# Re-planning a fused attention and two-layer gated network on one core: new lock rules, new matmul prices, new priorities

## The chip, the cores and the metric

The kernel runs on one core of a Trainium2 chip. The metric is the device time of one launch in microseconds (us), taken as the median of the runs. The engines are PE (TensorE; PEld is its weight load), DVE (VectorE), ACT (ScalarE), POOL (GpSimd) and SP (SyncE), which here issues the DMAs. Each engine works through its own instructions in program order.

## The reference

Three layers follow one another, in float32. B is 4, H is 8, S is 576, D is 64, the model width is 512 and the inner width is 1024.

```python
# 1: attention; heads 0 to 3 see the last 32 keys, heads 4 to 7 every fourth of the last 128
scores = np.where(masks, q @ k.T / 8, -1e9)
x = softmax(scores) @ v                      # (B, S, 512)
# 2: token shift, squared relu, gate
xk = mu_k * x + (1 - mu_k) * x_prev; xr = mu_r * x + (1 - mu_r) * x_prev
x = sigmoid(xr @ w_r) * (np.maximum(xk @ w_k, 0) ** 2 @ w_v)
# 3: spatial gate
h = np.maximum(x @ w_in, 0); u, v = h[..., :512], h[..., 512:]
v_s = einsum('ts,bsd->btd', w_spatial, layernorm(v)) + b_spatial
out = (u * v_s) @ w_out
```

## The kernel before

The four batches b go through attention in two halves each: `att(b, 0)` for the four plain heads, `att(b, 1)` for the four dilated ones. A half is cut into blocks of 32 queries by 64 keys, 18 blocks in the plain half and 20 in the dilated one, so 38 blocks in a batch, and three groups of them (6 or 8 blocks) form one softmax step: score matmuls (`scores`, four small float32 matmuls to a block, one for each head), a mask, maximum, subtraction, exponential, sum, reciprocal and product on DVE, ACT and POOL, then transposes and `values` on PE. In batch 0 every third score block is led by a matmul whose result nobody uses (`keep_warm`). A float32 matmul leaves two records in the trace, so 48 records of scores are 24 matmuls, or 6 blocks; 20 records of values are 5 groups.

Layer 2 takes a batch in two halves of 288 tokens (`moe1_k`, `moe1_r`, `moe1_v`), layer 3 a batch at a time (`moe2`). Their products run as three float32r matmuls to a term: high by high, high by low, low by high. The splits into high and low parts (`halves`, `split`, tiles xh and xl, kh and kl, gh and gl) are a copy on ACT or DVE and a subtraction on DVE or POOL. In batch 0 the first product uses w_k whole, in plain float32; w_k is split later (`split_whole`). Weights come as 64-bit words and are turned into float32 by two ACT instructions and one of DVE (`split_weight`), 512 KB to a load.

The order of all this is written by a planner that runs on the host before the program is built. Every piece of work is an `add(...)` with its cost on each engine that may do it, what it reads and writes, and whether it is a DVE instruction that competes with POOL (`two`, lines 194 on). `schedule` (lines 221 on) simulates the engines: it picks among the pieces that are ready the one with the lowest priority number, and puts it on the engine where it ends first, with a penalty for DVE or POOL. `begin` and `until` (lines 258 and 264) model the competition between DVE and POOL. `tuned` makes the priority from the table `TUNE`: for the k-th of n pieces of one kind it is the piece's own due number, plus the table's first entry, plus its second times k/n; the last two entries of four are the penalties in ns for DVE and for POOL.

`order` then walks through the planned PE work: where the plan has PE empty for over 60 ns in its first 100 us, it fills the hole with bf16 matmuls of ones (fillers; tile names const-bfloat16-1.0). The program issues everything in the planned order, so a plan that is wrong about a duration does not break the result, but an engine then waits for the next instruction of its queue while others further back could run. All engine instructions are issued through one helper, so all have line 453 in the profile; the tile names tell them apart.

Of the kernel before, what the change touches and what calls it, by code (L numbers as in the profile page):

```python
# [36 lines left out]
def blocks(dil):  # L37
# [39 lines left out]
    ('nat', 0): {'nat': (-290891, -21190, 792, 22)},  # L77
    ('nat', 1): {'nat': (-99107, 59817, 792, 22)},
    ('nat', 2): {'nat': (-2719, -33639, 792, 22)},
    ('nat', 3): {'nat': (6890, -14597, 792, 22)},  # L80
    ('nat', 4): {'nat': (6134, 3634, 792, 22)},
    ('out', 0): {'egh': (-5837, -69306, 792, -800), 'egl': (-4485, -5835, -200, 300), 'ot': (-6470, -41169, -200, 22), 'out': (-3506, -12993, 792, 22), 'psB': (4616, 30510, 792, 22)},
    ('out', 1): {'egh': (-5605, 46828, 400, -800), 'egl': (-9221, 34856, -600, -800), 'ot': (-5825, 55324, -200, 22), 'out': (-573, -83659, 792, 22), 'psB': (-3029, 10154, 792, 22)},
    ('out', 2): {'egh': (-6267, 4285, -600, 800), 'egl': (-4284, -14269, 1500, 22), 'ot': (-7057, -70234, -600, 22), 'out': (338, -35004, 792, 22), 'psB': (-6791, -32635, 792, 22)},
    ('out', 3): {'egh': (-10401, -19476, 400, 0), 'egl': (-6940, 7231, 0, 300), 'ot': (-13264, -90296, 792, 22), 'out': (-7211, 6394, 792, 22), 'psB': (-13665, 52592, 792, 22)},
# [27 lines left out]
    ('start',): {'ident': (2016, -146136, 792, 22), 'identb': (6831, -68258, 792, 22), 'mask': (5734, -40694, 400, 22), 'mask2': (-265553, -66203, 792, 22), 'pt': (1829, 75005, 200, 2000), 'xok': (8400, -23780, 792, 22)},  # L113
# [55 lines left out]
class Plan:  # L169
# [51 lines left out]
    def schedule(self, prio):  # L221
# [42 lines left out]
        def until(e, i, t, c):  # L264
# [6 lines left out]
            if h <= t:  # L271
                return t + c
# [1535 lines left out]
```

## Time and profile before

| what | us |
|---|---|
| median of 3 runs | 589.58 (586.85 to 592.04) |
| the profiled execution's own time | 587.68 |
| its span, first to last instruction | 585.9 |
| PE busy | 569.7 (97%), of which fillers 18.4 |
| DVE busy | 353.0 (60%) |
| ACT busy | 253.0 (43%) |
| POOL busy | 123.5 (21%) |

PE is busy nearly all the time, but the fillers count as busy, so the share alone does not say how much work is left to be moved. Read it by stage: up to about 12 us PE can only wait for the first inputs, up to 150 us attention of batches 0 and 1 and the preparation of weights run beside the first products, and from 150 us on PE works nearly without a break. The profile also gives the granted clock of TensorE for every stretch.

### The profile page before, as it was taken

What the parts mean: (1) busy time and instruction counts of PE and PEld (TensorE: products, weight loads), DVE (VectorE), ACT (ScalarE), POOL (GpSimd) and SP (SyncE); (2) the same over time, 40 slices, a digit from 0 to 9 for tenths busy, and PEclk for the clock granted to TensorE, in tenths of its full rate; (3) what the DMA queues carried; (4) which work ended last, traced back from release to release, by engine and by line L of the source; (5) the groups of instructions that cost most, each with busy time, mean ns of one, the idle gap of its engine ahead of it and who ended that gap; (6) DMA issues with size and microseconds to landing.
All of it is one profiled execution on the core that took longest, in us unless ns stands there. A gap on an engine that the chain in (4) does not pass through costs nothing.

```text
span 585.9 us, 12550 instructions
## 1 busy us (share of the span) xinstructions
PE 569.7 (97%) x5171; PEld 508.7 (87%) x5171; DVE 353.0 (60%) x745; ACT 253.0 (43%) x566; POOL 123.5 (21%) x146
## 2 busy tenths in 40 slices
PE   9999998998999999999999999999999999999996
PEld 5666786787989999999999999988988988889995
DVE  2889998898784779561616122789344616634440
ACT  4697845554263475734526162085123012303231
POOL 1313214345112211110400010042005301420030
PEclk9999999998999999999999999999999999999999
DMA  9999955687621444000000010230011001001002
GB/s 180 232 227 231 271 101 104 129 120 112 130 61 26 107 144 145 21 0 1 1 1 2 1 46 0 68 111 23 1 37 37 0 19 55 18 2 37 36 1 90
DMA packets 99513, 42.92 MB, mean 73 GB/s; under 512 B 86208, under 2 KB 92352, under 8 KB 99456
## 3 DMA queue, kind: packets, MB, share of 16 engines
q1 hardware_dynamic: 99456, 42.13, 32.3%
q8 instruction: 40, 0.66, 0.5%
q14 instruction: 17, 0.14, 0.1%
HBM read 37.39 MB, written 4.72 MB: 72 GB/s over the span
## 4 chain that ended last, share of the span: by engine, by line
PE 80%; DVE 11%; DMA 4%; SPq 2%; issue 2%; ACT 1%; POOL 0%; DVEq 0%; ACTq 0%; POOLq 0%
PE psM L453 55%; PE psB L453 15%; PE psT L453 7%; PE psS L453 2%; DMA ld<-in_k_dram 2%; SPq L453 2%; DVE st L453 1%; DVE pr L453 1%; DVE kT L453 1%; DMA raw<-in_moe_w_out_dram 1%; DVE xm L453 1%; DVE tmp L453 1%; DVE xd L453 1%; DVE sq_dt.float32r L453 1%; DVE qT L453 1%
## 5 line engine op out<-in xcount | busy, mean ns | idle before, releaser
L453 PE MATMUL psM<-xh,wk 128*128 128x288 f32 x512 | 122.0, 328 | 0.3 <-DVE x L453 0.3
L453 PE MATMUL psM<-sq_dt.float32r,wv 128*128 128x288 f32 x768 | 114.3, 299 | 0.2 <-DVE wv L453 0.2
L453 PEld LDWEIGHTS psM<-sq_dt.float32r,wv 128*128 128x128 f32 x768 | 105.4, 189 | 2.6 <-ACT x L453 0.7
L453 PEld LDWEIGHTS psM<-xh,wk 128*128 128x128 f32 x512 | 87.2, 188 | 8.6 <-DVE x L453 1.2
L453 PE MATMUL psM<-xh,wr 128*128 128x288 f32 x256 | 62.1, 303 | 2.4 <-ACT kr L453 1.4
L453 PE MATMUL psM<-x2h,wi 128*128 128x288 f32 x256 | 57.6, 298 | 0.0
L453 PE MATMUL psM<-xl,wk 128*128 128x288 f32 x192 | 56.6, 295 | 0.0
L453 DVE TENSOR_TENSOR sq_dt.float32r<-kr,sq_dt.float32r 128x288 fp32r<-128x288 f32 x57 | 29.1, 512 | 36.8 <-ACT sq_dt.float32r L453 36.5
L453 PEld LDWEIGHTS psM<-xh,wr 128*128 128x128 f32 x256 | 44.3, 189 | 4.6 <-ACT kr L453 2.4
L453 PEld LDWEIGHTS psM<-x2h,wi 128*128 128x128 f32 x256 | 43.1, 188 | 1.9 <-ACT u L453 1.1
L453 ACT ACTIVATE u<-psM 128x288 f32<-128x288 f32 x27 | 11.1, 411 | 76.2 <-PE psM L453 74.7
L453 ACT ACTIVATE kr<-psM 128x288 f32<-128x288 f32 x51 | 20.9, 410 | 48.8 <-PE psM L453 46.0
L453 POOL TENSOR_TENSOR xl<-xm,xh 128x288 fp32r<-128x288 f32 x23 | 20.1, 879 | 96.3 <-DVE xh L453 80.2
L453 PE MATMUL psB<-wi,x2h 128*128 128x512 f32 x128 | 40.4, 397 | 0.0
L453 PE MATMUL psB<-wo,gh 128*128 128x512 f32 x128 | 39.9, 393 | 0.0
L453 PE MATMUL psM<-wsh,vl 128*128 128x288 f32 x128 | 38.0, 297 | 1.1 <-DVE vl L453 1.1
L453 PE MATMUL psM<-x2l,wi 128*128 128x288 f32 x128 | 37.8, 295 | 0.9 <-DVE eps L453 0.9
L453 PE MATMUL psM<-xl,wr 128*128 128x288 f32 x128 | 38.1, 298 | 0.2 <-DVE xl L453 0.2
L453 PE MATMUL psM<-wsh,vh 128*128 128x288 f32 x128 | 38.0, 297 | 0.0
L453 PE MATMUL psM<-wsl,vh 128*128 128x288 f32 x128 | 37.7, 295 | 0.0
L453 PEld LDWEIGHTS psM<-xl,wk 128*128 128x128 f32 x192 | 36.1, 188 | 0.0
L453 DVE SCALAR_TENSOR_TENSOR xm<-xd,mu,x 128x288 f32<-128x288 f32 x56 | 32.1, 595 | 5.7 <-POOL xl L453 5.1
(155 smaller groups left out, 1119.6 us busy)
## 6 DMA issues: line engine op xcount, KB each, us to landing
vw<-in_v_dram SPq DMA_DIRECT2D x36, 128.0 KB, 3.1
room<-in_moe_w_k_dram SPq DMA_DIRECT2D x8, 512.0 KB, 9.4
room<-in_moe_w_v_dram SPq DMA_DIRECT2D x8, 512.0 KB, 6.0
raw<-in_moe_w_in_dram SPq DMA_DIRECT2D x8, 512.0 KB, 3.8
out_dram<-ot SPq DMA_DIRECT2D x16, 256.0 KB, 2.0
ld<-in_q_dram SPq DMA_DIRECT2D x48, 72.0 KB, 2.6
ld<-in_k_dram SPq DMA_DIRECT2D x48, 72.0 KB, 3.2
vw<-in_v_dram SPq DMA_DIRECT2D x8, 288.0 KB, 5.5
```

The lines of the kernel that those rows point to most:

```text
L453: return self.tc.keep_in_program_order(getattr(self.engine, name)(*args, **kw))
```

## The change

Three things change in the planner; no instruction of the program is added, taken away or reshaped, except that fillers, which engine a piece goes to, and the order follow from the plan.

First, the competition of DVE and POOL: before, the later of two overlapping instructions ran on at 0.4 (POOL) or 0.35 (DVE) of its speed; some kinds ("both") waited for POOL to end. Now every DVE instruction marked `two` starts no sooner than 56 ns ahead of the end of the POOL instruction in hand, and a POOL instruction no sooner than 130 ns ahead of the end of such a DVE instruction. Second, a block of scores is put at 130 ns instead of 190 (batches 1 to 3) and 160 instead of 260 (batch 0), a group of values at 146 instead of 155. Third, all 109 entries of the table of priorities and penalties have new numbers.

```diff
         def begin(e, i):
             t = max(free[e], at[i])
-            if e == "dve" and two[i] == "both":
-                t = max(t, held["pool"])
+            if e == "dve" and two[i]:
+                t = max(t, held["pool"] - 56)
+            elif e == "pool" and i not in self.far:
+                t = max(t, held["dve"] - 130)
             return t
 
         def until(e, i, t, c):
-            if e == "pool":
-                h, rate = held["dve"], 0.4
-            elif e == "dve" and two[i]:
-                h, rate = held["pool"], 0.35
-            else:
-                return t + c
-            if h <= t:
-                return t + c
-            return t + c / rate if c / rate <= h - t else h + c - (h - t) * rate
+            return t + c
...
-            if e == "pool" or e == "dve" and two[i]:
+            if e == "pool" and i not in self.far or e == "dve" and two[i]:
                 held[e] = end
...
-                {"pe": m * (190 if b else 260) + (w_ / 2.4 if pe_mask else 0)}, scores,
+                {"pe": m * (130 if b else 160) + (w_ / 2.4 if pe_mask else 0)}, scores,
...
-                    {"pe": 155 * (g1 - g0)}, values,
+                    {"pe": 146 * (g1 - g0)}, values,
...
-    ('nat', 3): {'nat': (6890, -14597, 792, 22)},
-    ('nat', 4): {'nat': (6134, 3634, 792, 22)},
-    ('vw', 0, 0): {'vw': (4704, 20869, 792, 22)},
-    ('w', 'wk', 'ld'): {'raw': (4260, 21829, 792, 22)},
+    ('nat', 3): {'nat': (11393, -58910, 792, 22)},
+    ('nat', 4): {'nat': (9806, 3564, 792, 22)},
+    ('vw', 0, 0): {'vw': (11897, 30528, 792, 22)},
+    ('w', 'wk', 'ld'): {'raw': (5601, 28533, 792, 22)},
...
```

## Rows read from the trace of the kernel before

**Rows 1.** The page's head and PE's busy time.
```profile
span 585.9 us, 12550 instructions
PE 569.7 (97%) x5171; PEld 508.7 (87%) x5171; DVE 353.0 (60%) x745; ACT 253.0 (43%) x566; POOL 123.5 (21%) x146
```

**Rows 2.** Stretches: length, busy time (instructions) of PE, PEld, DVE, ACT, POOL, granted clock, DMA.
```profile
12.00:50.00 38.00, 37.21 (x539) 23.86 (x527) 31.29 (x70) 28.33 (x54) 11.49 (x13) 1.00 1.12 222
50.00:90.00 40.00, 37.91 (x348) 31.28 (x347) 39.46 (x73) 27.20 (x56) 8.99 (x10) 1.00 0.90 197
90.00:150.00 60.00, 54.95 (x936) 45.66 (x936) 52.68 (x106) 30.30 (x72) 27.62 (x29) 0.97 0.70 117
150.00:586.00 436.00, 428.39 (x3272) 401.89 (x3270) 227.50 (x496) 161.75 (x378) 74.40 (x87) 1.00 0.14 40
580.00:586.00 6.00, 1.31 (x6) 0.75 (x4) 0.00 (x0) 0.59 (x1) 0.00 (x0) 0.86 0.32 89
```

**Rows 3.** The fillers and the keep-warm matmuls among PE's groups: count, busy us, mean ns.
```profile
L453 PE MATMUL psT<-const-bfloat16-1.0 128*128 128x512 bf16 x64 | 18.4, 411 | 0.8 <-PEq L1791 0.8
L453 PE MATMUL psT<-const-bfloat16-1.0,identb 128*128 128x512 bf16 x13 | 5.0, 384 | 0.0
```

**Rows 4.** Both of them by stretch (PE busy, PEld, POOL, clock, DMA).
```profile
12.00:50.00 38.00, 12.45 (x41) 2.62 (x30) 0.00 (x0) 1.00 1.12 222
50.00:90.00 40.00, 1.44 (x5) 0.33 (x5) 0.00 (x0) 1.00 0.90 197
```

**Rows 5.** PE's waits between 90 and 150 us: total, times, longest (one of four rows).
```profile
PE psT L453 <- DVE pr L453: 1.7, 1, 1.7
```

**Rows 6.** PE's order of time around 135 us, where the clock fell: start, length, instruction.
```profile
136.72 1.01 PE L453 MATMUL psT<-pt,vw 128*64 128x64 f32 x20 [1.90 <-DMA vw<-in_v_dram]
137.66 1.81 PE L453 MATMUL psM<-sq_dt.float32r,wv 128*128 128x288 f32 x6
140.92 1.07 PE L453 MATMUL psM<-sq_dt.float32r,wv 128*128 128x288 f32 x6
```

**Rows 7.** The chain that ended last, batch 1 to 3: six score blocks, five value groups.
```profile
147.71 0.80 PE psS L453 x48
143.61 0.73 PE psT L453 x20
```

**Rows 8.** PE's order of time, batch 0: six plain blocks, then eight dilated ones.
```profile
10.57 0.38 PE L453 MATMUL psT<-const-bfloat16-1.0,identb 128*128 128x512 bf16 x1
12.14 1.09 PE L453 MATMUL psM<-ident,early 128*128 128x128 f32 x8
...
15.68 0.38 PE L453 MATMUL psT<-const-bfloat16-1.0,identb 128*128 128x512 bf16 x1
18.94 1.09 PE L453 MATMUL psM<-ident,early 128*128 128x128 f32 x8
```

**Rows 9.** POOL and DVE in order of time: three POOL splits, DVE beside them and alone.
```profile
34.91 0.45 DVE L453 TENSOR_TENSOR xd<-x 128x288 f32<-128x288 f32 x1
...
95.88 0.56 DVE L453 TENSOR_TENSOR pr<-pr,st 128x384 f32<-128x384 f32 x1
100.04 4.51 POOL L453 TENSOR_TENSOR wk<-wk,wk 128x512 fp32r<-128x512 f32 x3 [0.55 <-PE psM L453]
100.36 1.62 DVE L453 TENSOR_TENSOR pr<-pr,st 128x384 f32<-128x384 f32 x1
```

**Rows 10.** DVE's groups between 90 and 150 us: busy us, mean ns.
```profile
L453 DVE TENSOR_TENSOR pr<-pr,st 128x384 f32<-128x384 f32 x8 | 5.8, 727 | 0.1
L453 DVE TENSOR_TENSOR xd<-x 128x288 f32<-128x288 f32 x5 | 4.3, 854 | 0.0
```

**Rows 11.** SP's order of time, the first loads: start, length, DMA issued.
```profile
7.63 1.12 SPq L453 DMA_DIRECT2D vw<-in_v_dram  x1
8.79 2.14 SPq L453 DMA_DIRECT2D early<-in_q_dram  x2
...
12.57 1.62 SPq L453 DMA_DIRECT2D room<-in_moe_w_k_dram  x3
```

More of the change, by code (lines that the diff above doesn't have):

```diff
@@ L56 @@
 TUNE = {
[20 rows of a table removed]
-    ('nat', 0): {'nat': (-290891, -21190, 792, 22)},
-    ('nat', 1): {'nat': (-99107, 59817, 792, 22)},
-    ('nat', 2): {'nat': (-2719, -33639, 792, 22)},
-    ('nat', 3): {'nat': (6890, -14597, 792, 22)},
-    ('nat', 4): {'nat': (6134, 3634, 792, 22)},
-    ('out', 0): {'egh': (-5837, -69306, 792, -800), 'egl': (-4485, -5835, -200, 300), 'ot': (-6470, -41169, -200, 22), 'out': (-3506, -12993, 792, 22), 'psB': (4616, 30510, 792, 22)},
-    ('out', 1): {'egh': (-5605, 46828, 400, -800), 'egl': (-9221, 34856, -600, -800), 'ot': (-5825, 55324, -200, 22), 'out': (-573, -83659, 792, 22), 'psB': (-3029, 10154, 792, 22)},
@@ L84 @@
-    ('out', 2): {'egh': (-6267, 4285, -600, 800), 'egl': (-4284, -14269, 1500, 22), 'ot': (-7057, -70234, -600, 22), 'out': (338, -35004, 792, 22), 'psB': (-6791, -32635, 792, 22)},
-    ('out', 3): {'egh': (-10401, -19476, 400, 0), 'egl': (-6940, 7231, 0, 300), 'ot': (-13264, -90296, 792, 22), 'out': (-7211, 6394, 792, 22), 'psB': (-13665, 52592, 792, 22)},
[27 rows of a table removed]
-    ('start',): {'ident': (2016, -146136, 792, 22), 'identb': (6831, -68258, 792, 22), 'mask': (5734, -40694, 400, 22), 'mask2': (-265553, -66203, 792, 22), 'pt': (1829, 75005, 200, 2000), 'xok': (8400, -23780, 792, 22)},
[12 rows of a table removed]
@@ L126 @@
-    ('val', 0, 0): {'psT': (4544, -156816, 792, 22), 'x': (8940, 35148, 1500, 22)},
-    ('val', 0, 1): {'psT': (7975, 110348, 792, 22), 'x': (6866, 28781, -200, 22)},
-    ('val', 1, 0): {'psT': (2174, -26451, 792, 22), 'x': (5281, -49395, 792, 22)},
-    ('val', 1, 1): {'psT': (-1354, -41077, 792, 22), 'x': (2396, -66321, -200, 22)},
-    ('val', 2, 0): {'psT': (-110, 65622, 792, 22), 'x': (1033, 119822, -200, 22)},
-    ('val', 2, 1): {'psT': (657, 11731, 792, 22), 'x': (2917, -58124, 1500, 22)},
@@ L132 @@
-    ('val', 3, 0): {'psT': (-2740, 3159, 792, 22), 'x': (-1208, -12655, 1500, 22)},
-    ('val', 3, 1): {'psT': (2149, -11387, 792, 22), 'x': (6222, 102527, 400, 22)},
[26 rows of a table removed]
-    ('ws',): {'bb': (-4458, -40090, 792, 22), 'psB': (-4008, 6385, 792, 22), 'raw2': (-4569, 104472, 792, 22), 'wsh': (366, 64678, -600, 22), 'wsl': (-2359, 196419, 792, 22), 'wslz': (-1250, -18099, 792, 22), 'wst': (-8171, 28426, 792, 22)},
[5 rows of a table removed]
[20 rows of a table added]
+    ('nat', 0): {'nat': (-329879, -19907, 792, 22)},
+    ('nat', 1): {'nat': (-299721, 92338, 792, 22)},
@@ new lines @@
+    ('nat', 2): {'nat': (-3613, -38466, 792, 22)},
+    ('nat', 3): {'nat': (11393, -58910, 792, 22)},
+    ('nat', 4): {'nat': (9806, 3564, 792, 22)},
+    ('out', 0): {'egh': (-4691, -72671, 400, 0), 'egl': (-7305, -798, -200, 22), 'ot': (-12300, -35652, 200, 22), 'out': (-4066, -143572, 792, 22), 'psB': (18521, 40071, 792, 22)},
+    ('out', 1): {'egh': (-5939, 74800, 792, -800), 'egl': (-5927, 61520, -200, 2000), 'ot': (-4330, 127985, -600, 22), 'out': (-8230, -96426, 792, 22), 'psB': (-5643, 429, 792, 22)},
@@ new lines @@
+    ('out', 2): {'egh': (-5515, -61457, -600, 800), 'egl': (-6225, -12309, 1500, -800), 'ot': (-7541, -84174, 1500, 22), 'out': (-11103, -8388, 792, 22), 'psB': (-5954, -40576, 792, 22)},
+    ('out', 3): {'egh': (-5768, 23373, 400, 2000), 'egl': (-7474, 20186, 400, 800), 'ot': (-6843, -92606, 1500, 22), 'out': (-5954, -28246, 792, 22), 'psB': (-5189, 60236, 792, 22)},
[27 rows of a table added]
+    ('start',): {'ident': (3089, -108430, 792, 22), 'identb': (9847, -36570, 792, 22), 'mask': (9223, -114599, 400, 2000), 'mask2': (-329887, -133537, 792, 22), 'pt': (1605, 136576, 792, -300), 'xok': (5876, -21465, 792, 22)},
[12 rows of a table added]
@@ new lines @@
+    ('val', 0, 0): {'psT': (6190, -188538, 792, 22), 'x': (7908, 41361, 200, 22)},
+    ('val', 0, 1): {'psT': (4893, 102845, 792, 22), 'x': (7841, 33477, 400, 22)},
+    ('val', 1, 0): {'psT': (9587, -71450, 792, 22), 'x': (870, -18001, 200, 22)},
+    ('val', 1, 1): {'psT': (-572, -56085, 792, 22), 'x': (-8750, -66130, 792, 22)},
+    ('val', 2, 0): {'psT': (1125, 52007, 792, 22), 'x': (-748, 147378, 1500, 22)},
+    ('val', 2, 1): {'psT': (247, 7891, 792, 22), 'x': (92, -74319, 400, 22)},
+    ('val', 3, 0): {'psT': (-3199, -3823, 792, 22), 'x': (-788, -23971, -200, 22)},
@@ L166 @@
+    ('val', 3, 1): {'psT': (557, -9155, 792, 22), 'x': (432, 58129, 400, 22)},
[26 rows of a table added]
+    ('ws',): {'bb': (-624, -45651, 792, 22), 'psB': (-932, 3281, 792, 22), 'raw2': (-5575, 87056, 792, 22), 'wsh': (-1850, 27434, -600, 22), 'wsl': (-2755, 197422, 792, 22), 'wslz': (-2256, -26649, 792, 22), 'wst': (-4221, 34122, 792, 22)},
[5 rows of a table added]
 }
```

176 rows, old and new, of the table TUNE are left out of this document.

## The prediction

> **What bounds the kernel now.** I read the page's head first [rows 1]: PE is busy 569.7 of 585.9 us, so the end is set by PE, and the change can win only where PE is empty or does work that nobody needs. The second sort is in PE's groups [rows 3]: the fillers take 18.4 us and the keep-warm matmuls 5.0. The table by stage [rows 2] then tells where the empty time lies. From 12 to 50 us PE is idle 38.00 - 37.21 = 0.8 us, from 50 to 90 it is 2.1, from 90 to 150 it is 60.00 - 54.95 = 5.05, and in all of the 436 us after that 7.6, of which 6.00 - 1.31 = 4.7 is the way of the last output after the last matmuls. So the long second part has only 2.9 us to give. The same table by the fillers' tile [rows 4] adds 12.45 us between 12 and 50 us and 1.44 between 50 and 90; of the 12.45, 11 keep-warm matmuls are 11 x 0.384 = 4.2, which stay, and 8.2 are fillers. The first 12 us wait for the first inputs and are left alone here.
>
> In the stages with room, DVE is the next bound: it is busy 39.46 of 40 us between 50 and 90 and 52.68 of 60 between 90 and 150 [rows 2]. PE's waits between 90 and 150 name a softmax product of DVE for 1.7 us [rows 5], and PE's order of time there names a load of v for 1.9 us [rows 6]. Beside that wait the granted clock falls: over 90 to 150 us it is 0.97 [rows 2], and the six matmuls right behind the wait take 1.81 us, six of the same kind later 1.07 [rows 6]. That is the step from 2.4 to 1.2 GHz for a few us: 0.74 us on these six, and 1.01 - 0.73 = 0.28 on the 20 value records before them [rows 6, 7], so about 1.0 us.
>
> **The change, part by part.** The work is the same, so each term is the change of a wait.
>
> *Lock of DVE and POOL.* The rows show what it is about. A product of 128x384 takes DVE 0.56 us with no POOL work beside it and 1.62 us when it starts inside a row of three POOL splits of 4.51 / 3 = 1.50 us each [rows 9]. The old rule stretches it by 1 / 0.35 and gives 0.56 / 0.35 = 1.60 us, almost what is seen. The new rule has it start when POOL ends, 1.50 - 0.3 us later, and gives about 1.7. The two rules differ by at most 0.35 of the time that DVE is held. The largest hold is one POOL instruction: 0.35 x 1.50 = 0.5 us, and with the mean POOL instruction between 90 and 150 us, 27.62 / 29 = 0.95 us [rows 2], it is at most 0.33, and half of that where the start falls anywhere in it. The 29 POOL instructions of that stage thus leave the old plan wrong by up to 29 x 0.17 = 4.8 us of DVE time, if each holds a DVE instruction once. What contention costs there today can be bounded from the means: 8 products at 727 instead of 560 ns and 5 differences xd at 854 instead of 450 [rows 9, 10] are 1.3 + 2.0 = 3.3 us in two kinds. No row says how much of it a better order takes away; the ends are nothing and all of it.
>
> The Trainium skill has the rule that the new plan adopts (SBUF — State Buffer, "SBUF: two separate sides"): the port pair shared by DVE and GpSimd is an exclusive lock, held for the whole instruction, and the other side blocks entirely. The row of 1.62 us agrees. By that rule the old plan was optimistic by the 0.17 us a hold worked out above, by a rule of shared speed it was exact and this part of the change would be worth nothing; that second case is rival 1.
>
> *Prices of scores and values, batches 1 to 3.* Six blocks take 0.80 us, 134 ns each, and five value groups 0.73 us, 146 each [rows 7]. The old plan had 190 and 155, the new one 130 and 146. Over 3 x 38 = 114 blocks the old plan held PE for 114 x 56 = 6.4 us that don't exist. PE then comes early to its next instruction and waits for what DVE was told it had time for. The new plan can put product matmuls there. A third of the blocks, batch 1's, lies in the stage from 74 to 150 us where PE has its gaps.
>
> *Stage 90 to 150.* Together these two can win at most the 5.05 us of idle time and the 1.0 of clock, 6.0. The wait for v is a matter of the queue of loads, whose prices did not change, so 1.9 and the clock behind it I leave in. Of the other 5.05 - 1.9 = 3.15 I take 2.5, since DVE's contention of 3.3 us is of the same size. From the other side, a new order can place one wait more like the longest seen: +1.9.
>
> *Stage 50 to 90.* Room 2.1 + 1.44 = 3.5 us. DVE is full (39.46 of 40), and an order does not make its work less unless POOL is used at better times. I take -1.0, between -3.5 and, by the same longest wait, +1.9.
>
> *Prices of scores, batch 0.* Here the new number is farther from the trace. Six plain blocks with their two keep-warm matmuls take from 10.57 to 12.14 us, 262 ns a block; eight dilated ones from 15.68 to 18.94, 408 a block [rows 8]. At 260 the plan was short by 20 x 148 = 3.0 us, at 160 it is short by 18 x 102 + 20 x 248 = 6.8. The additional 3.8 us look to the plan like empty PE time, and `order` fills it with ones, which then push the real scores back. The cover is that PE holds 8.2 us of fillers up to 50 us [rows 3, 4] while it waits for DVE, ACT and weights; if the cover is gone, it costs +3.8. On the other end the new order may close some of the holes: I bound that gain by half of the 8.2, 4.1 us. I take +0.5.
>
> *First loads.* Priorities in the table's terms: before, the first block of w_k has 331 - 398 + 4260 = 4193 and stands behind the last q and k pieces of batch 0 (1893 for piece 3, 2955 for piece 4's k) and the first v (-246). After, it has 5534 and stands ahead of piece 3's q (6396), piece 4's k (6592) and the first v (6947). SP's order before agrees: v, then q and k, then w_k from 12.57 us on [rows 11]. One block is 512 KB, at 222 GB/s [rows 2] an estimated 2.4 us of load time ahead of inputs that the dilated scores need. What is queued behind it on SP is the rest of the inputs; what waits is the last transposes on PE and then all dilated scores. w_k comes no later in return. Between 0 and +2.4 I take +0.5, since PE is in plain scores and fillers then.
>
> *After 150 us.* 2.9 us of waits can go, as many can come: -0.5, between -2.9 and +2.9.
>
> **Sum.** 587.68 (the profiled execution: span 585.9 and 1.8 around it) - 2.5 - 1.0 + 0.5 + 0.5 - 0.5 = 584.7. The median of the runs is 1.9 above the profiled execution, which lies low among them; carried over in full the sum would be 586.6. I forecast 585.0.
>
> **Rivals.** Rival 1, no change: the old stretched speed already fits the one measured hold (1.60 against 1.62), the waits left are loads and a full DVE, and what one stage wins the next one gives back. For it: DVE at 39.46 of 40. Against it: 6.4 us of PE time that the old plan imagined. Time 587 to 591.
>
> Rival 2, slower: the underpriced scores of batch 0. Place: 12 to 30 us. Price: 3.8 us of additional fillers if the plan stays as long, and up to the whole 6.8 us of wrong price if DVE and ACT, which follow PE's scores, are then out of step with their queues. It decides as soon as PE's fillers before 50 us grow instead of shrink, and DVE, full up to 90 us, cannot catch up: 587.68 + 3.8 to 6.8 is 591.5 to 594.5 in the profiled execution's terms, 593.4 to 596.4 in the median's.
>
> Rival 3, a larger gain: the order also removes the load wait with the slow clock (2.9 us) and a third of the 8.2 us of fillers (2.7), on top of the sum: 585.0 - 5.6 = 579.4.
>
> **How the numbers follow.** Forecast (582 to 587): 0.42. Rival 1: 0.25. Rival 2: 0.17. Rival 3: 0.16. 585.0 is that of the forecast. About 1% is what a measurement of this kernel can tell from no change, since three runs spread over 5 us. 1% below the median is 583.7, which takes all of rival 3 and rather more than half of the forecast's lower side, 0.24 of 0.42: faster 0.40. Above 595.5 lies most of rival 2 with its bounds added: slower 0.13. The rest, 0.47, is within 1%. The range goes from 577, below rival 3, to 593, which leaves out rival 2's upper part; the forecast's own range is 582 to 587.
>
> **What would show it.** Right: idle PE time from 90 to 150 us under 3 us; fewer DVE products beside POOL, their mean nearer 560 than 727; PE's waits for softmax products gone. Wrong: more than 41 filler and keep-warm matmuls between 12 and 50 us (rival 2); the transposes of the last inputs later than 18.94 us by 2 us or more (first loads); new waits in the 436 us after 150, where I allow 2.9. The forecast fails altogether if batch 1's attention, with its loads, starts later, for all later work hangs on it.

## The result

| | before | changed |
|---|---|---|
| median of 13 runs, us | 589.87 (586.85 to 596.0) | 582.88 (581.66 to 587.59) |
| ratio, 95% interval | 1 | 0.9893 (0.9873 to 0.9914) |
| profiled execution: time / span, us | 587.68 / 585.9 | 581.66 / 579.9 |

The changed kernel is 1.1% faster, 7.0 us by the medians and 6.0 by the two profiled executions, inside the forecast's own range. First the page of the changed kernel: PE's busy time, and the chain that ended last by engine.

```profile
PE 568.5 (98%) x5186; PEld 510.2 (88%) x5196; DVE 353.1 (61%) x768; ACT 252.7 (44%) x559; POOL 111.2 (19%) x130
...
PE 94%; DVE 2%; ACT 2%; issue 1%; DMA 1%; POOL 0%; DVEq 0%; ACTq 0%
```

The chain of the kernel before, and that of a second profile of the changed kernel (changed_again below):

```profile
PE 80%; DVE 11%; DMA 4%; SPq 2%; issue 2%; ACT 1%; POOL 0%; DVEq 0%; ACTq 0%; POOLq 0%
```
```profile
PE 84%; DVE 5%; DMA 4%; SPq 3%; ACT 2%; issue 1%; DVEq 0%; ACTq 0%
```

Busy PE time hardly moved (569.7 to 568.5, [rows 1]). The way to the end led through PE for 80% of the span; in the changed kernel it does so for 94% in one profile and 84% in the other, so this share is too unsteady to rest anything on. PE's idle time is 579.9 - 568.5 = 11.4 us (10.5 in the second profile), before 16.2. Next the stretches of the changed kernel (columns as in [rows 2]), and the fillers and keep-warm matmuls from 12 to 50 us (as in [rows 4]) in its two profiles.

```profile
12.00:50.00 38.00, 35.06 (x493) 21.52 (x491) 25.70 (x56) 26.26 (x50) 9.37 (x11) 1.00 1.00 227
50.00:90.00 40.00, 39.38 (x382) 32.60 (x384) 37.58 (x73) 29.14 (x63) 10.21 (x13) 1.00 0.89 189
90.00:150.00 60.00, 58.84 (x980) 50.41 (x980) 51.79 (x107) 31.84 (x75) 26.18 (x26) 1.00 0.66 116
```
```profile
12.00:50.00 38.00, 14.90 (x53) 4.61 (x50) 0.00 (x0) 1.00 1.00 227
```
```profile
12.00:50.00 38.00, 17.32 (x61) 4.60 (x50) 0.00 (x0) 1.00 0.97 223
```

From 90 to 150 us PE idles 1.16 us instead of 5.05 and the clock stays at 1.00. But from 12 to 50 us it is worse. Both profiles are of one program, and both show 50 weight loads of fillers there, so the first lacks 8 matmul records of fillers and keep-warm; counts of all other matmuls agree. By the second, 61 fillers and keep-warm matmuls stand there instead of 41, and PE idles 38.00 - 36.19 = 1.81 us instead of 0.79 (2.94 in the first profile, for want of those records). PE's waits from 90 to 150 us are down to one row (before [rows 5]), DVE's softmax products there are shorter (before [rows 10]; the differences xd too, 667 ns instead of 854), and the values that stood behind the load of v ([rows 6]) now run without a wait:

```profile
PE psT L447 <- DVE pr L447: 1.0, 1, 1.0
```
```profile
L447 DVE TENSOR_TENSOR pr<-pr,st 128x384 f32<-128x384 f32 x8 | 4.5, 582 | 0.0
```
```profile
136.06 0.80 PE L447 MATMUL psT<-pt,vw 128*64 128x64 f32 x20
```

Idle time alone does not tell how far PE has come, because fillers are busy time too and small pieces with pauses between them count as busy to their modelled ends. So I counted work: the records of each kind of matmul in a stretch, fillers and keep-warm left out, times the length of one where PE runs without a break. Three such runs of the kernel before set the main prices: 759 matmuls of 288 columns in 101.11 us are 133 ns each, 63 of 512 columns in 14.47 us are 230, and 38 records of the float32 product with the whole w_k in 9.84 us are 259. Scores and values are from [rows 7], 17 and 37 ns a record; transposes and masks are put at 110 to 180.

```profile
263.29 101.11 PE psM L453 x759
```
```profile
48.00 9.84 PE L453 MATMUL psM<-xh,wk 128*128 128x288 f32 x38
```

PE work done, in us, from the first instruction to the time at the head. All kernels of this text end between 539.7 and 540.8.

| by | 50 | 90 | 150 | 250 | 365 | 410 |
|---|---|---|---|---|---|---|
| before | 26.0 | 61.4 | 113.5 | 209.7 | 324.7 | 367.9 |
| changed | 20.4 | 57.4 | 115.7 | 213.8 | 328.5 | 374.3 |
| ahead by | -5.6 | -4.0 | +2.2 | +4.1 | +3.8 | +6.4 |

This is the story of the 6 us: 5.6 lost by 50 us, 1.6 regained by 90, 6.2 won between 90 and 150, 1.9 between 150 and 250, 2.6 between 365 and 410 where layer 3 begins, nothing after. The second profile of the changed kernel gives 20.3, 57.5, 115.5, 212.8, 327.6 and 373.0, so differences of about 1 us in this table say nothing; after 150 us it makes the gain 3.1 us and not 4.2.

### The profile page after: what moved, and what is told of

It is laid out like the page before. It is cut to its first block, busy times and chain, and to the rows that moved or that the text cites. A ratio compares the mean times of both kernels' runs of the same rounds, so it can differ in the third digit from the quotient of the medians.

```text
span 579.9 us, 12622 instructions
## 1 busy us (share of the span) xinstructions
PE 568.5 (98%) x5186; PEld 510.2 (88%) x5196; DVE 353.1 (61%) x768; ACT 252.7 (44%) x559; POOL 111.2 (19%) x130
## 4 chain that ended last, share of the span: by engine, by line
PE 94%; DVE 2%; ACT 2%; issue 1%; DMA 1%; POOL 0%; DVEq 0%; ACTq 0%
PE psM L447 65%; PE psB L447 17%; PE psT L447 8%; PE psS L447 4%; DMA room<-in_moe_w_v_dram 1%; ACT pt L447 1%; DVE pt L447 0%; DVE kr L447 0%; DVE pr L447 0%; DVE x2h L447 0%; ACT wk L447 0%; ACT vw L447 0%; DVE vt L447 0%; ACT x2h L447 0%; DVE wk L447 0%
## 5 line engine op out<-in xcount | busy, mean ns | idle before, releaser
L447 PE MATMUL psM<-xh,wr 128*128 128x288 f32 x256 | 63.3, 307 | 0.3 <-ACT kr L447 0.3
L447 POOL TENSOR_TENSOR xl<-xm,xh 128x288 fp32r<-128x288 f32 x32 | 29.2, 918 | 69.9 <-ACT xh L447 45.7
L447 DVE SCALAR_TENSOR_TENSOR x<-x,psM 128x288 f32<-128x288 f32 x32 | 14.3, 452 | 39.9 <-PE psM L447 33.4
L447 ACT CAST sq_dt.float32r<-kr 128x288 fp32r<-128x288 f32 x44 | 19.0, 433 | 40.4 <-DVE kr L447 27.4
L447 DVE SCALAR_TENSOR_TENSOR xm<-xd,mu,x 128x288 f32<-128x288 f32 x56 | 30.8, 569 | 6.1 <-POOL xl L447 5.8
L447 ACT ACTIVATE kr<-psM 128x288 f32<-128x288 f32 x45 | 18.3, 409 | 33.2 <-PE psM L447 30.1
```

The lines of the kernel that those rows point to most:

```text
L447: return self.tc.keep_in_program_order(getattr(self.engine, name)(*args, **kw))
```

## The experiments

### Which part carries the gain

The two halves of the change were first taken apart as they stand: new rules and prices with the old table, and the new table with the old rules.

```diff
 # rules_old_table: the changed kernel
-TUNE = { ...new... }
+TUNE = { ...old... }
 # table_old_rules: the kernel before
-TUNE = { ...old... }
+TUNE = { ...new... }
```

> The changed kernel's lock rule and prices with the priorities and penalties of the kernel before. If the gain of 7 us comes from the rules themselves, this keeps most of it: 582 to 586 us. If the table is what carries it, and a table fits only the rules under which it was made, this is no faster than before: 590 to 600 us, with new PE waits between 90 and 150 us.

> The kernel before with the new table of priorities and penalties, old lock rule and old prices. If the new table alone carries the gain: 582 to 586 us. If table and rules belong together: 590 to 605 us, since the plan that comes out was never weighed as a whole.

Measured: rules_old_table 594.34 us, ratio to before 1.0082 (1.0054 to 1.011); table_old_rules 602.56 us, 1.0209 (1.0167 to 1.0252). Each half alone is slower than before. rules_old_table loses most between 130 and 150 us, where PE is busy 13.80 of 20 us, before 18.10.

A table fits the rules under which it was made. So in what follows a table goes with each set of rules: its entries were changed at random and a change kept where the plan's own end came earlier or little later, for the same time, from the old table. Lock and prices are then told apart by this edit, with both together as the control.

```diff
 # prices_only: the kernel before, table adjusted
-                {"pe": m * (190 if b else 260) + ...
+                {"pe": m * (130 if b else 160) + ...
-                    {"pe": 155 * (g1 - g0)}, values,
+                    {"pe": 146 * (g1 - g0)}, values,
 # lock_only: the kernel before, begin / until / held of the changed kernel, table adjusted
 # both_retuned: both of these, table adjusted
```

> The kernel before with the new prices of scores and values and its old rule for DVE and POOL; its table was adjusted anew under these, from the old one. If prices and lock each carry a part (my theory): 584.5 to 587 us, that is a third to two thirds of the 7 us. If the prices carry all of it, since the old stretched speed fitted the measured hold of 1.62 us: 581.5 to 584 us. If only the lock matters: 588 to 591 us, no change.

> The kernel before with the new rule for DVE and POOL and the old prices; table adjusted anew under these, from the old one. If each carries a part: 584.5 to 587 us. If the prices carry all: 588 to 592 us, no faster than before. If the lock carries all: 581.5 to 584 us.

> Both new rules with a table adjusted anew from the old one, in the same way and for as long as the two single ones; the control for them. If the rules are the cause and not the particular new table: 580 to 585 us, as the changed kernel. If the gain is the luck of one table: 587 to 592 us.

| run | us | ratio to before (95%) |
|---|---|---|
| prices_only | 585.16 | 0.9916 (0.9887 to 0.9946) |
| lock_only | 592.8 | 1.0037 (1.0005 to 1.007) |
| both_retuned | 584.06 | 0.9888 (0.9827 to 0.995) |

My theory, that each carries a part, falls: prices_only lies in the range that it gave, but lock_only is slower than all three ranges named for it. The new lock rule alone gives nothing, rather a loss of 0.4%; the prices alone give three quarters of the control's gain by the ratios, and the two intervals overlap. both_retuned is as fast as the changed kernel (0.9893), so the gain is no luck of one table. What was not run is the kernel before with its old rules and prices and its table adjusted anew; lock_only, and early_scores_only below, adjusted under a change that brings nothing, come nearest to it. The stretch from 90 to 150 us, lock_only and then prices_only:

```profile
90.00:150.00 60.00, 53.90 (x939) 44.66 (x942) 48.26 (x106) 27.49 (x66) 29.32 (x31) 1.00 0.62 107
```
```profile
90.00:150.00 60.00, 57.92 (x901) 49.99 (x900) 51.12 (x98) 29.35 (x69) 27.30 (x30) 1.00 0.66 113
```

PE idles 6.1 us under the new lock rule with old prices and 2.1 under the old rule with new prices. Yet in lock_only the softmax products of this stage are as short as one without POOL work beside it (0.56 us, [rows 9]; the mean before was 727 ns):

```profile
L447 DVE TENSOR_TENSOR pr<-pr,st 128x384 f32<-128x384 f32 x3 | 1.6, 549 | 0.0
```

### Which price

The new prices are two: batches 1 to 3, where the new number is the trace's, and batch 0, where it is farther from it than the old one. Each was changed alone, the old lock rule and the old price of values kept, the table adjusted from the old one.

```diff
 # late_scores_only
-                {"pe": m * (190 if b else 260) + ...
+                {"pe": m * (130 if b else 260) + ...
 # early_scores_only
+                {"pe": m * (190 if b else 160) + ...
```

> The kernel before with one number changed, the price of a score block in batches 1 to 3, 130 ns for 190, and the table adjusted anew from the old one. If the 6.4 us that the old plan held PE for nothing are the cause: 583.5 to 586.5 us, all that the new prices gave (0.9916 of before). If the price of batch 0 is the cause: 588 to 592 us.

> The kernel before with the price of a score block of batch 0 at 160 ns for 260, and the table adjusted anew from the old one. If this price is the cause of the gain: 583.5 to 586.5 us. If, as I hold, it is only a wrong price: 589 to 593 us, more fillers before 50 us and less real PE work by 50 us than before.

Measured: late_scores_only 583.25 us, 0.9868 (0.9827 to 0.9908); early_scores_only 590.26 us, 0.9986 (0.9959 to 1.0012). One number, 130 for 190, is worth as much as the whole change. Taken over all kernels of this text with a table of their own, the six with 130 are at 0.9791 to 0.9916 of before, the two with 190 (lock_only and early_scores_only) at 1.0037 and 0.9986. From 90 to 150 us, late_scores_only and then early_scores_only:

```profile
90.00:150.00 60.00, 58.53 (x874) 51.79 (x873) 46.18 (x85) 28.25 (x68) 31.49 (x34) 1.00 0.54 100
```
```profile
90.00:150.00 60.00, 55.86 (x766) 47.99 (x765) 46.48 (x91) 29.81 (x70) 21.32 (x21) 0.97 0.52 92
```

In late_scores_only the softmax products did not get rid of POOL. They are longer there than before (727, [rows 10]), and POOL is busier (31.49 us against 27.62), yet PE idles 1.5 us only:

```profile
L453 DVE TENSOR_TENSOR pr<-pr,st 128x384 f32<-128x384 f32 x5 | 4.1, 830 | 0.1
```

So the gain comes without shorter products here, and in lock_only shorter products come without a gain: those of the changed kernel (582) are not its cause. By 50 us late_scores_only has 25.7 us of work done, as before (26.0); by 150 us it has 118.1, against 113.5. A lag up to 50 us comes with the other price: early_scores_only has 21.3 us by 50, and 64 fillers and keep-warm matmuls between 12 and 50 us:

```profile
12.00:50.00 38.00, 17.96 (x64) 4.70 (x51) 0.00 (x0) 1.00 1.01 213
```

### What causes the lag up to 50 us in the changed kernel

Two suspects could be taken out of the finished order without any new plan: the first load of w_k, and the fillers behind 29 us.

```diff
 # load_order: in order(), behind self.schedule
+        kinds = [self.tags[i] for _, i, _ in self.out]
+        first = next(j for j, k in enumerate(kinds) if k == ("w", "wk", "ld"))
+        last = ...   # the last of the q, k and first v loads of batch 0
+        self.out.insert(last, self.out.pop(first))
 # no_fill_30_50: the condition for fillers
-                if start < 100000 and start - end > 60:
+                if start < 29000 and start - end > 60:
```

> The changed kernel with one instruction moved: the first load of w_k is issued behind the last q and k pieces of batch 0 and the first v, as before; the rest of the order is untouched. If the loss of PE work up to 50 us (5 to 6 us behind the kernel before) starts at the late inputs and is carried to the end: 580.0 to 581.5 us, ratio to before 0.985 to 0.987, and the last input transposes 2 us earlier than 22.7 us. If later stages (DVE, w_r and w_v loads) absorb it: within 0.7 us of the changed kernel, ratio 0.988 to 0.990.

> The changed kernel without the 30 fillers that the plan puts behind its 29th us; nothing else moves. If the fillers hold up real work between 30 and 50 us (rival 2's mechanism): 579.5 to 581.5 us. If PE waits there for softmax on DVE and ACT anyway: within 0.7 us of the changed kernel, with the fillers' time turned into idle time. If the clock falls without them: slower by 1 to 4 us, with a granted clock under 1.00 between 30 and 60 us.

Measured: load_order 582.46 us, 0.9881 (0.9849 to 0.9913), no difference from the changed kernel. The last input transposes did not even move forward. Those of the kernel before, the changed kernel and load_order:

```profile
20.30 0.93 PE L453 MATMUL psM<-ident,early 64*128 64x64 f32 x8
```
```profile
22.70 0.46 PE L447 MATMUL psM<-ident,early 64*128 64x64 f32 x4 [0.46 <-ACT turned L447]
```
```profile
23.33 0.46 PE L451 MATMUL psM<-ident,early 64*128 64x64 f32 x4 [0.45 <-ACT turned L451]
```

In the changed kernel and load_order they stand behind dilated scores and fillers in PE's queue, and at their end they wait for ACT, not for a load. no_fill_30_50 came out slower than the changed kernel: 584.66 us, 0.9938 (0.9911 to 0.9965). Of the 30 fillers that it lacks, 20 stood before 50 us and 10 behind. Two of its stretches:

```profile
35.00:40.00 5.00, 3.00 (x47) 2.35 (x49) 4.45 (x12) 4.22 (x10) 1.10 (x1) 0.80 0.94 215
90.00:150.00 60.00, 55.22 (x890) 46.44 (x888) 48.91 (x98) 29.23 (x69) 21.45 (x22) 1.00 0.60 110
```

From 35 to 45 us PE works 3.0 to 3.2 of 5 us and waits for softmax pieces, and the granted clock is 0.80 to 0.86, a mean of 1.2 and 2.4 GHz, in every 5 us stretch from 35 to 65 us; with fillers it is 1.00. This profile is of the slowest of eight executions (588.53 us, mean clock 0.989). The four with 0.997 took 583.8 to 584.3 us, the four with 0.985 to 0.991 took 585.0 to 588.5, so the time goes with the clock. Between 90 and 150 us PE idles 4.8 us at a clock of 1.00, against 1.16, so in the profiled execution the clock is not all of the loss. Fillers at this place thus hold up little and more than pay for themselves; they are worth about 2 us (1.8 by the medians, 0.45% by the ratios, whose intervals just touch). The Trainium skill (TensorE: Matmul & The Clock Gate, "Why this matters for your kernels") advises against idle gaps of PE between bursts of matmuls, since the clock drops; this run agrees, with its 0.80.

Next came the wrong price of batch 0 itself, which makes the plan mistake the time of everything around it. It was put right in the changed kernel, and the table adjusted anew; the second run has a table adjusted for a longer time.

```diff
-                {"pe": m * (130 if b else 160) + ...
+                {"pe": m * (130 if b else 408 if dil else 262) + ...
```

> Both new rules, and the scores of batch 0 at what the trace of before shows, 262 ns a plain block and 408 a dilated one in place of 160; table adjusted anew in the same way. If the wrong price of batch 0 costs the changed kernel its lag of 5 us up to 50 us: 577 to 580.5 us, fewer fillers between 12 and 50 us and over 22 us of real PE work by 50 us. If the lag comes from DVE and ACT in that stage: 581.5 to 585 us.

> Both new rules, batch 0's scores at 262 and 408 ns a block, the table adjusted for a longer time than in the run with true prices. If the true price of batch 0 is worth something over the changed kernel: 578 to 581.5 us, clear of it. If the first run's 582.0 was only within the noise of the changed kernel: 581.5 to 584 us, no difference.

> The changed kernel, untouched, on the same chip as the other three, for the comparison with them: 582 to 584 us, ratio to before 0.987 to 0.991.

| run | us | ratio to before (95%) |
|---|---|---|
| b0_price_true | 582.02 | 0.9866 (0.9797 to 0.9934) |
| b0_price_true_longer | 578.34 | 0.9791 (0.9754 to 0.9827) |
| changed_again, same chip | 583.69 | 0.9889 (0.9846 to 0.9932) |

The first is faster than the changed kernel by less than its interval; it has 23.6 us of work by 50 us, as expected, but its time lies in the range of the other expectation (581.5 to 585). The second beats both kernels: 12.8 us under the one before, 5.4 under the changed one, and the intervals do not meet. It has 40 fillers and keep-warm matmuls between 12 and 50 us instead of 61, and 23.7 us of work by 50 us instead of 20.4, 59.9 by 90 instead of 57.4, 117.6 by 150 instead of 115.7.

What is not told apart here: how much of the 5.4 us is the price and how much the longer adjusting, since the changed kernel's table was not adjusted further under its own prices. The two tables under the same rules and prices lie 3.7 us apart by the medians, so one table is a rough measure of a rule. Nor is it settled that the wrong price makes the lag by 50 us. Over all kernels with a table of their own it stands so, with the fillers counted by their weight loads (the profiles of changed, lock_only, prices_only, both_retuned and b0_price_true lack 9 to 13 matmul records of fillers and keep-warm):

| price of a block in batch 0 | work by 50 us | weight loads of fillers, 12 to 50 us |
|---|---|---|
| 160 (changed, early_scores_only, prices_only, both_retuned) | 20.4, 21.3, 22.1, 23.7 | 50, 51, 48, 47 |
| 260 (before, late_scores_only, lock_only) | 26.0, 25.7, 22.8 | 30, 32, 43 |
| 262 and 408 (b0_price_true, longer) | 23.6, 23.7 | 32, 29 |

Every kernel with 160 has more fillers than any other: a price too low makes the plan see holes that are not there. The work by 50 us tells less. Under the old lock rule 260 gives 26.0 and 25.7, 160 gives 21.3 and 22.1; under the new one 260 gives 22.8, 160 gives 20.4 and 23.7. So lock_only, with the price of before, loses 3.2 us by 50 us and has 13 fillers more: the new lock rule is a second suspect for the lag, and no run tells the two apart.

## Why the prediction was right or wrong

The forecast (585.0, its own range 582 to 587) held: 582.88, near the range's lower end. The largest chance, 0.47, had gone to a time within 1% of before; with 0.9893 (0.9873 to 0.9914) it came out just beyond that line, with an interval that reaches across it. The mechanism was half right, and three of the terms had the wrong size.

**What bounds the kernel.** Right. All the time was won where PE had been idle or badly fed; the tail after the last matmul (4.6 us in both traces) is as it was. Mis-sized was the part after 150 us: I took -0.5 and allowed 2.9 by its idle time, and PE gained 6.4 - 2.2 = 4.2 there, 3.1 by the second profile. Whether the bound of 2.9 was broken, two profiles that far apart do not settle. Which piece of the plan won the 2.6 us between 365 and 410 us was not tried.

**Lock of DVE and POOL.** Wrong as a cause. I gave the lock and the prices the 2.5 us of the stage together, on the ground that DVE's contention of 3.3 us was of that size. The lock rule alone made nothing faster (1.0037), and the price alone did it with more contention than before. Rival 1 had the right outcome for this part, and a wrong reason: that the old stretched speed fits the chip. The row of 1.62 us fits both rules (1.60 and 1.7) and settles nothing. The next one in the same trace does:

```profile
101.90 1.52 DVE L453 TENSOR_TENSOR xd<-x 128x288 f32<-128x288 f32 x1
```

A difference xd takes 0.45 us alone [rows 9]; at 0.35 of its speed it would end after 1.29 us at the latest. It took 1.52 and ended at 103.42, about 0.4 us after the second of the three POOL splits [rows 9] (100.04 + 2 x 1.50 = 103.04). So it was held until POOL had done and then ran at full speed: that is the exclusive lock that the Trainium skill states (SBUF — State Buffer, "SBUF: two separate sides"), and this row agrees. So the new lock rule is nearer to the chip, and still a plan with it did not order its work any better. Why not, no run shows.

**Prices of scores, batches 1 to 3.** Right, and mis-sized. The price behind the 6.4 us of PE time that the old plan imagined is the cause (late_scores_only), and the stage from 90 to 150 us won 6.2 us of work where I took 2.5 of at most 6.0. I had left the wait for v and the slow clock behind it in, 2.9 us, because the loads' prices were untouched. But a new order moves loads too; both are gone in the changed kernel, while early_scores_only still has a clock of 0.97 there. The condition "idle under 3 us" came true with 1.16.

**Stage 50 to 90.** -1.0 forecast, 1.6 measured.

**Prices of scores, batch 0, and rival 2.** The place and the sign were right, and the size was too small: +0.5 taken, +5.6 measured by 50 us. The signal I named for rival 2 came: 61 fillers and keep-warm matmuls instead of 41. Rival 2 still failed, at its second condition: the lag was made good, 1.6 us of it by 90 us and the rest between 90 and 150. Its mechanism was wrong in one respect. I had the additional fillers push real scores back; taking 30 fillers out cost time instead of giving any. With load and fillers excluded, the order that follows from the price, the new lock rule or both are left as its cause; the table of kernels above does not decide.

**First loads.** +0.5 taken, nothing measured (0.9881 against 0.9893). The last input transposes came 1.5 to 2 us later (from 20.30, against 21.78 and 22.70), about what I had said would show this step, but putting the load back did not bring them forward. The sign was a poor one: another cause, the scores and fillers ahead of them in PE's queue, moves it as well.

**Rival 3** came by half: the wait for v and the slow clock are gone, but the fillers grew.

**The sum** came near by luck, because errors cancelled: the loss up to 50 us was 4.6 us larger than the +1.0 of its two terms, the gains 0.6 and 3.7 larger in the next two stages and 3.7 after 150: -3.0 + 4.6 - 0.6 - 3.7 - 3.7 = -6.4, about twice the -3.0 that I had summed. The sum missed by 3.0 us (584.7 against 581.66 for the profiled execution), the forecast of the median by 2.1.

## What to carry to other kernels

When a planner writes the order, look first for a price that is wrong on the engine that bounds the kernel: here 56 ns too much on 114 blocks of scores was worth 1%, and a better model of a port lock beside it was worth nothing. Each change of a rule or a price needs a new table before it is judged; taken with the old one, the rules of this change measured 0.8% slower instead of 1.1% faster. Measure a price at every place where it is used: batch 0 and the dilated half took 262 and 408 ns where one number of 160 stood, and putting them right with more adjusting gave another 1%.

## What the runs showed of the hardware

Scores that read every fourth element (dilated, batch 0) take longer than plain ones. Behind one keep-warm matmul each, 24 records of dilated scores take 0.85 us in the changed kernel and 24 of plain scores 0.47, at the same granted clock of 1.00 and with the same shapes. The step between elements is the difference that the kernel's text shows; it was not tried by itself.

```profile
14.67 0.85 PE psS L447 x24
...
24.51 0.47 PE psM L447 x24
```

And 30 filler matmuls, whose results nobody uses, are worth about 2 us of the whole run; without them the granted clock falls to 0.80 to 0.86 for 30 us, which is part of that, if not all.
